# Folding x a second time, and the last transform product over the two halves of the array's rows

## The chip, the core and the metric

The kernel runs on one core of a Trainium2 chip. A core has a matrix engine (TensorE, "PE", with its weight loads shown apart as "PEld"), VectorE ("DVE"), ScalarE ("ACT"), GpSimd ("POOL") and SyncE ("SP"), which run side by side and wait for one another through semaphores. Data come from the chip's memory by DMA into SBUF; TensorE reads SBUF and writes PSUM[...]. The metric is the device time of one launch in microseconds, lower is better.

## What is computed

The reference is a Fourier mixing layer followed by a mixture-of-experts layer in which every token goes to one expert:

```python
def _attn_ref(x):                       # x: (8, 2496, 256), float32
    X = np.fft.fft(x, axis=1)
    X = np.fft.fft(X, axis=2)
    return X.real.astype(np.float32)

def _moe_ref(x, w_gate, w1, w2):        # x: (19968, 256), 8 experts, F = 1024
    logits = x @ w_gate
    expert_idx = np.argmax(logits, axis=1)
    ...
    gate_w = probs[np.arange(N), expert_idx]
    ...
    for e in range(E):
        lo, hi = (boundaries[e], boundaries[e + 1])
        h = np.maximum(x_sorted[lo:hi] @ w1[e], 0.0)
        y_sorted[lo:hi] = h @ w2[e]
    y = y_sorted[inv_perm]
    return (gate_w[:, None] * y).astype(np.float32)
```

`probs` is the softmax of the logits. The sequence length is 2496 = 104 x 24, so the transform along it is done in two steps, of 104 (`NA`) and of 24 (`NB`).

## The kernel before

The eight batches pass through a pipeline. While the experts work on the tokens of batch b - 1, the transform of batch b and the first stage of batch b + 1 are woven in between as side work.

**First stage** (`first`, `fold`, `fold_d`, `half1`). A batch's x comes in three thirds, each a tile `xq` of 104 partitions with eight rows of 256 numbers; three such tiles are in rotation (`xp`, tag `xq`). `fold` (L294) first adds the four mirrored rows of n2 to the other four (L301), then `fold_d` (L287) folds along d: positions 1 to 127 become the sum of d and 256 - d, positions 129 to 255 their difference, and 0 and 128 are copied (L290 to L292). These are VectorE operations. In the last third one row, `pm0`, is folded apart. `half1` (L306) multiplies the folded rows by the table `w1` over 104 partitions, ACT copies the product from PSUM (L316), and a DMA on SP or ACT writes it to `Td` in memory (L337), from where `regroup` (L346) reads it back with other rows on the partitions.

**Second stage** (`second`, L356). 53 positions of the sequence's spectrum (`NK`) are left after the fold, five to a group, so there are 11 groups (`NG`) in a batch. `turn_last(h)` (L360) turns one column of the regrouped tile `t4` by a small product with the table `rot` (tile `pr`) and copies the result back on ACT; there are two such tiles a batch. `group(g)` (L369) takes two products, over 120 partitions and with 120 columns, into a PSUM tile `p2`, and ACT copies it into `zz` (L374). In `zz` the partitions are the 128 folded positions of d, once for each of two parts c.

**Last stage**, the row product (loop at L391). Ten steps a batch (`NW`, 80 in the kernel) each take 128 columns of `zz` as weights and multiply them with the table `rd` into a PSUM tile `p3`: one product for each part c, over all 128 partitions and with 145 and 146 columns. The columns hold the half spectrum along d (129 values, `NY`), the gate's logits for two mirrored rows (2 x 8) and one column for the last position. ACT copies the second part to `zs` (L400). VectorE copies the logits out of `p3` (L403) and makes the two mirrored rows, as `p3 + last +/- zs` (L405). `mirror` (L378), on ACT, fills the other half of each row. After five steps `route` (L411) finds each row's expert and its place, and `send` (L457) lets POOL write each row to `Xs` by an indirect DMA (L230).

**Buffers.** `p2`, `p3`, the product of `half1`, `pr` and the small products of `route` share three PSUM buffers (`pm_`, tag `m`, `bufs=3`); the experts have the five others (`pse`).

**Experts** (`experts`, L627). Blocks of up to 512 rows are fetched from `Xs` with their expert's weights. Each is transposed (`pt`, L571) and multiplied with w1 (tiles a to e in blocks that use seven products in place of eight, `ph` in the others), then with w2 (`py`), scaled (L721) and scattered to the output (L230). At the end of the last round some blocks may be empty; `needed` (L635) then does a one-row product of ones in place of the block's work.

**The order** is written out by hand (`tc.manual_schedule()`). The loop at L824 draws from `experts` and, for the work that each step reports, lets so many ticks of the side work fall due:

```python
            if not full:
                due += TICKS * w / (SHARE * open_) if w else 1
            while due >= 1:
                next(side, None)
                due -= 1
                if b < LATE or not w:
                    send()
```

`TICKS` is 32 (L183) and `SHARE` 0.6. A tick is what lies between two `yield`s of `mixed` (L764), which advances `second(b)` by one step, and after every other step `first(b + 1)` as well. For batch 0 there is no expert work to weave with: its first stage, the first stage of batch 1 and its second stage run by themselves.

The tables are built on the host in `shape_consts` (L57): `rt`, `rd` and `alt` (a sign for each of 128 positions, by which the transposed rows are scaled at L572) depend on how d is folded.

Of the kernel before, what the change touches and what calls it, by code (L numbers as in the profile page):

```python
# [22 lines left out]
H = D // 2  # L23
# [16 lines left out]
ROWS = E * CAP + BLK  # L40
W = D + 2
NSL = 2 * HW
NY = H + 1
OUT = 1.0e6


def free(ap, offset, *dims):
    return bass.AP(ap.tensor, ap.offset + offset, [list(ap.ap[0])] + [list(d) for d in dims])
# [8 lines left out]
def shape_consts():  # L57

    c = {}
    n1 = np.arange(NA)[:, None]  # L60
    r = np.arange(NP)
    k1 = r // 2
    im = r % 2

    def wave(n2, f):
        return f(2 * np.pi / S * ((NB * n1 + n2) * k1 % S))

    w1 = [np.where(im, wave(n2, np.sin), wave(n2, np.cos)) for n2 in range(1, NS)]
    for f in (np.cos, np.sin):
        w1 += [np.where(im, 0.0, wave(0, f)), np.where(im, wave(NS, f), 0.0)]  # L70
    c["w1"] = np.stack(w1, 1) * (k1 < NK)

    u, cs, s = np.meshgrid(np.arange(NU), np.arange(2), np.arange(NS), indexing="ij")
    u, cs, s = (v.reshape(-1, 1) for v in (u, cs, s))
    k2 = np.arange(NB)
    t = 2 * np.pi / NB * ((s + 1) * k2 % NB)
    end = np.where(cs, 1.0 - 2.0 * (k2 % 2), 1.0)
    even = np.where(s == NS - 1, end, np.where(cs, -np.sin(t), np.cos(t)))
    odd = np.where(s == NS - 1, end, np.where(cs, np.cos(t), np.sin(t)))
    own = (u == np.arange(NU)).astype(float)  # L80
    c["m2"] = np.stack([(own[:, :, None] * m[:, None, :]).reshape(GP, GP) for m in (even, odd)], 1)

    rot = np.zeros((GP, GP))
    for p in range(GP):
        if p % NS == NS - 1:
            rot[p, p] = 1.0
        elif p // NS % 2:
            rot[p, p - NS] = -1.0
        else:
            rot[p, p + NS] = 1.0  # L90
    c["rot"] = rot

    d = np.arange(H)[:, None]
    m = np.arange(D + 1)
    t = 2 * np.pi / D * (d * m % D)
    rc, rs = np.cos(t), -np.sin(t)
    rs[0] = 1.0 - 2.0 * (m % 2)
    full = np.concatenate([rc[:, :D], rs[:, :D]], 0)


    rd = np.zeros((H, 2, 2 * E + NY + 1))
    sign = 1.0 - 2.0 * (m[:NY] % 2)
    rd[:, 0, 0:NY] = sign * rc[:, 0:NY]
    rs[0] = 0.0
    rd[0, 1, 2 * E] = 1.0
    rd[:, 1, 2 * E + 1:] = sign * rs[:, 0:NY]
    c["rd"] = rd
    c["alt"] = 1.0 - 2.0 * (np.arange(128) % 2)[:, None]
    c["rt"] = full.T.reshape(2, 128, D).transpose(1, 0, 2)

    p = np.arange(128)[:, None, None, None]
    h = np.arange(2)[None, :, None, None]
    g = np.arange(HW)[None, None, :, None]
    mir = np.arange(2)
    tau = 128 * (HW * h + g) + p
    k1 = tau // NB
    k = k1 + NA * (tau % NB)
    bad = (k1 >= NK) | ((mir == 1) & ((k1 == 0) | (k1 == NK - 1)))
    row = np.where(bad, 0, np.where(mir, S - k, k))
    c["row"] = row.reshape(128, 2, NSL)  # L120
    c["good"] = 1.0 - bad.reshape(128, 2, NSL)
    c["far"] = OUT * bad.reshape(128, 2, NSL)
    c["rev"] = np.broadcast_to(E - np.arange(E), (128, E))
    c["cap"] = np.broadcast_to(CAP * np.arange(E), (128, E))
    c["sgn"] = np.where(np.arange(128) == 0, 1.0, -1.0)[:, None]
    c["lane"] = np.arange(128)[:, None]
    c["tri"] = np.triu(np.ones((128, 128)), 1)
    c["ident"] = np.eye(128)
    return {n: np.ascontiguousarray(v, dtype=np.float32) for n, v in c.items()}
# [50 lines left out]
    return todo  # L180


TICKS = 32  # L183
LATE = 4
SHARE, ROOM = 0.6, 1.2
WARM = 16
# [23 lines left out]
def kernel(ctx: ExitStack, tc, x, w_gate, w1, w2, out):  # L210
# [3 lines left out]
    def mm(o, lhsT, rhs, start=True, stop=True, **kw):  # L214
        nc.tensor.matmul(o, lhsT=lhsT, rhs=rhs, start=start, stop=stop, **kw)  # L215
# [71 lines left out]
    def fold_d(o, a, n):  # L287

        lo, hi = free(a, 1, [D, n], [1, H - 1]), free(a, D - 1, [D, n], [-1, H - 1])
        vec.tensor_tensor(free(o, 1, [D, n], [1, H - 1]), lo, hi, op=ALU.add)  # L290
        vec.tensor_tensor(free(o, H + 1, [D, n], [1, H - 1]), lo, hi, op=ALU.subtract)
        vec.tensor_copy(free(o, 0, [D, n], [H, 2]), free(a, 0, [D, n], [H, 2]))  # L292

    def fold(xq, q, pm0):  # L294

        a, m = xq[:, 0:4], xq[:, 4:8]
        n = 4
        if q == NQ - 1:
            n = 3
            fold_d(pm0, m[:, 3], 1)  # L300
        vec.tensor_tensor(a[:, 0:n], a[:, 0:n], m[:, 0:n], op=ALU.add)  # L301
        yield
        fold_d(m, a, 4)
        yield

    def half1(b, q, half, pm, pm0, t1):  # L306
# [13 lines left out]
    def first(b):  # L320

        pm0 = xp.tile([NA, D], F32, tag="pm0", name="pm0")
        for q in range(NQ + 1):
            f = iter(())
            if q < NQ:
                xq = ahead.pop((b, q))
                f = fold(xq, q, pm0[:])
            next(f, None)
            yield
            if q:  # L330
                t1 = xp.tile([NP, 4, D], F32, tag="t1", name="t1")
                half1(b, q - 1, 0, pm, pm0, t1)
            next(f, None)
            yield
            if q:
                half1(b, q - 1, 1, pm, pm0, t1)
                (nc.sync if b > 1 else act).dma_start(out=Td[b][:, 4 * (q - 1) * D:4 * q * D], in_=t1[:].rearrange("p j d -> p (j d)"))  # L337
                if b:
                    load(b + 1, q - 1)
            next(f, None)  # L340
            pm = xq[:, 4:8]
            yield

    base = con["cap"]
# [11 lines left out]
    def second(b):  # L356

        t4 = None

        def turn_last(h):  # L360

            nonlocal t4
            t4 = ahead.pop((b, "t4", h))
            n = min(HALF, NG - h * HALF)
            pr = pm_.tile([GP, HALF], F32, tag="m", name="pr")
            mm(pr[:, 0:n], con["rot"][:], t4[0:GP, 0:n, H])
            act.copy(t4[0:GP, 0:n, H], pr[:, 0:n])  # L367

        def group(g):  # L369
            i, n = g % HALF, LAST if g == NG - 1 else GP  # L370
            p2 = pm_.tile([128, 2, n], F32, tag="m", name="p2")
            for c in range(2):
                mm(p2[:, c], t4[0:GP, i, c * H:(c + 1) * H], con["m2"][:, c, 0:n])
            act.copy(zz[:, :, g * GP:g * GP + n], p2[:])  # L374
            if g == HALF - 1:
                turn_last(1)

        def mirror(rows, k):  # L378
            act.copy(free(rows[:], (k + 1) * W + D - 1, [-W, 2], [-1, H - 1]),
                     free(rows[:], k * W + 1, [W, 2], [1, H - 1]))  # L380

        turn_last(0)
        yield
        group(0)
        yield
        group(1)
        yield
        for h in range(2):
            rows = sp.tile([128, NSL, W], F32, tag="rows", name="rows")
            lg = sp.tile([128, NSL, E], F32, tag="lg", name="lg")  # L390
            for i in range(HW):  # L391
                w, k = HW * h + i, 2 * i
                if w + 2 < NG:
                    group(w + 2)
                p3 = pm_.tile([128, 2 * NY + 2 * E + 1], F32, tag="m", name="p3")
                z = zz[:, :, 128 * w:128 * (w + 1)]
                mm(p3[:, 0:NY + 2 * E], z[:, 0], con["rd"][:, 0, 0:NY + 2 * E], True, False, skip_group_check=True)
                mm(p3[:, NY:], z[:, 1], con["rd"][:, 1], False, True, skip_group_check=True)
                zs = sp.tile([128, NY + 1], F32, tag="zs", name="zs")
                act.copy(zs[:], p3[:, NY + 2 * E:])  # L400
                if i:
                    mirror(rows, k - 2)
                vec.tensor_copy(lg[:, k:k + 2], p3[:, NY:NY + 2 * E].rearrange("p (m e) -> p m e", m=2))  # L403
                for m, op in enumerate((ALU.add, ALU.subtract)):
                    vec.scalar_tensor_tensor(rows[:, k + m, 0:NY], p3[:, 0:NY], zs[:, 0:1], zs[:, 1:],  # L405
                                             op0=ALU.add, op1=op)
                yield
            mirror(rows, k)
            yield from route(b, h, rows, lg)
# [354 lines left out]
    def mixed(b):  # L764

        one, two = (ahead_of(b + 1) if b + 1 < B else iter(())), second(b)
        for _ in range(3):
            next(one, None)
            yield
        for k, _ in enumerate(two):  # L770
            if k % 2:
                next(one, None)
            yield
        yield from woven(close(b), one)
        yield from through(b)
# [129 lines left out]
```

## Time and profile before

| | us |
|---|---|
| median of three runs | 1346.6 |
| lowest, highest | 1344.01, 1350.37 |
| the profiled execution | 1317.19 |
| its span, first to last instruction | 1314.9 |

The profiled execution is a single one and lies under the timed runs; what is counted up from its trace is compared with its own time. Its mean granted TensorE clock was 0.978 of full speed. A line of the trace gives the start and the duration in microseconds, the engine, the line of the kernel, the operation, the tile written and the tiles read, their shape, and a count if several of the kind follow one another. In the chain of waits, each line is a piece of the chain of work that ended last. All matrix work is recorded at L215, the helper `mm`, so its lines are told apart by the tiles. Each float32 product appears as two matmul instructions with two weight loads. Durations of matmuls overlap, since they are pipelined; what one costs is seen from start to start.

The work of the parts that the change touches, by the groups of the trace:

| what | count | mean, ns |
|---|---|---|
| row product, 145 and 146 columns (`p<-table,zz`) | 160 and 160 | 310 and 294 |
| group product, 120 columns (`p<-table,t`) | 320 | 291 |
| ACT copy to `zs` (L400), 128x130 | 80 | 268 |
| DVE logits (L403), 128x16 | 80 | 173 |
| DVE rows (L405), 128x129 | 160 | 343 |
| DVE fold along d (L290, L291), 104x508 | 24 and 24 | 683 and 679 |

### The profile page before, as it was taken

To read this page: it belongs to the slowest core of one execution; us is meant where nothing else is said; L and a number is where in the kernel's file an instruction comes from. 1 tells how busy PE (TensorE), PEld (TensorE's weight loads), DVE (VectorE), ACT (ScalarE), POOL (GpSimd) and SP (SyncE) were. 2 spreads that over 40 slices of the span, in tenths; PEclk is the share of its full clock that TensorE was granted. 3 is DMA by queue.
4 is the path that set the end of the run, shared out by engine and by line. 5 is a ranking of instruction groups with operands and counts; after the bars stand their busy time and mean duration, and the time that the engine had idled before them with its cause. 6 is when DMAs were issued, how large, how long until landed. Compare 5 with 4: busy or idle time off the path is not lost.

```text
span 1314.9 us, 19479 instructions
## 1 busy us (share of the span) xinstructions
PE 1270.8 (97%) x6823; PEld 1105.0 (84%) x6823; DVE 620.8 (47%) x1610; ACT 386.4 (29%) x907; POOL 330.6 (25%) x335
## 2 busy tenths in 40 slices
PE   5769999999999999999999999999999999999998
PEld 4659988776888888888888888888888889999887
DVE  4654253352656535664556644575544342222442
ACT  1422141231244223433334322432332231212221
POOL 0336125043114411153112511144211111111111
PEclk6869999999999999999999999999999999999999
DMA  8878967455436522574332633243432237777785
GB/s 245 268 240 302 389 213 247 160 171 188 182 134 205 199 104 97 176 267 131 145 111 81 244 115 105 97 159 133 155 138 101 97 133 262 277 270 260 274 324 196
DMA packets 63101, 249.65 MB, mean 190 GB/s; under 512 B 10057, under 2 KB 24883, under 8 KB 43420
## 3 DMA queue, kind: packets, MB, share of 16 engines
q1 hardware_dynamic: 46231, 203.33, 44.5%
q0 software_dynamic: 15888, 42.14, 8.8%
q10 hardware_dynamic: 885, 2.94, 0.7%
q8 instruction: 55, 0.90, 0.3%
q14 instruction: 42, 0.34, 0.1%
HBM read 194.97 MB, written 54.83 MB: 190 GB/s over the span
## 4 chain that ended last, share of the span: by engine, by line
PE 91%; issue 1%; DMA 1%; DVE 1%; ACT 0%; POOL 0%; POOLq 0%; SPq 0%; ACTq 0%
PE py L215 42%; PE ph L215 12%; PE c L215 8%; PE a L215 8%; PE p L215 5%; PE b L215 4%; PE e L215 4%; PE d L215 4%; PE pt L571 3%; PE s L215 2%; DMA xb<-Xs 0%; PE rk L215 0%; DMA Xs<-rows,pi 0%; DVE xq L301 0%; ACT y L721 0%
## 5 line engine op out<-in xcount | busy, mean ns | idle before, releaser
L215 PE MATMUL py<-w_sb,hT 128*128 128x256 f32 x2560 | 578.0, 380 | 0.0
L215 PEld LDWEIGHTS py<-w_sb,hT 128*128 128x128 f32 x2560 | 477.8, 190 | 60.5
L230 POOL DMA_INDIRECT out_dram<-y,ro x163 | 160.5, 985 | 806.4 <-ACT y L721 699.3
L721 ACT ACTIVATE y<-py,xb 128x256 f32<-128x256 f32 x163 | 77.2, 474 | 494.7 <-PE py L215 494.3
L230 POOL DMA_INDIRECT Xs<-rows,pi x160 | 162.1, 1013 | 172.4 <-DVE rows L405 52.7
L215 PE MATMUL ph<-xT,w_sb 128*128 128x128 f32 (+2 forms) x992 | 170.8, 328 | 2.9 <-ACT y L721 2.1
L215 PEld LDWEIGHTS ph<-xT,w_sb 128*128 128x128 f32 x992 | 136.6, 192 | 27.9 <-issue 17.2
L698 DVE TENSOR_SCALAR hT<-ph 128x512 f32<-128x512 f32 x49 | 33.9, 691 | 226.9 <-PE ph L215 109.9
L604 DVE TENSOR_TENSOR u<-p,b 128x512 f32<-128x512 f32 x57 | 39.2, 688 | 188.7 <-PE b L215 173.7
L215 PE MATMUL a<-xT,w_sb 128*128 128x256 f32 (+1 forms) x512 | 117.4, 356 | 0.0
L215 PEld LDWEIGHTS a<-xT,w_sb 128*128 128x128 f32 x512 | 89.7, 190 | 10.3
L572 DVE TENSOR_SCALAR xT<-pt,table 128x512 f32<-128x512 f32 (+1 forms) x94 | 63.3, 674 | 49.4 <-PE pt L571 49.2
L614 ACT ACTIVATE hT<-a 128x512 f32<-128x512 f32 x57 | 34.0, 597 | 152.1 <-PE a L215 152.1
L215 PE MATMUL s<-xq,w 104*112 104x256 f32 (+2 forms) x208 | 61.9, 421 | 11.8 <-DVE xq L292 11.3
L403 DVE COPY lg<-p 128x16 f32<-128x16 f32 x80 | 13.8, 173 | 120.2 <-ACT zs L400 120.1
L571 PE MATMUL pt<-table,xb 128*128 128x128 f32 x326 | 53.6, 280 | 9.4 <-DMA xb<-Xs 9.4
L215 PEld LDWEIGHTS p<-table,t 120*128 120x128 f32 x352 | 54.1, 203 | 9.1 <-issue 2.4
L215 PE MATMUL p<-table,zz 128*128 128x145 f32 (+1 forms) x320 | 57.0, 302 | 3.7 <-DVE rows L405 2.8
L215 PE MATMUL p<-table,t 120*128 120x120 f32 (+1 forms) x352 | 57.9, 289 | 1.7 <-ACT t L367 1.1
L215 PE MATMUL b<-xs,ws 128*128 128x256 f32 (+1 forms) x256 | 58.7, 356 | 0.0
L215 PE MATMUL d<-xT,w_sb 128*128 128x256 f32 (+1 forms) x256 | 58.7, 356 | 0.0
L215 PE MATMUL e<-xs,w_sb 128*128 128x256 f32 (+1 forms) x256 | 58.7, 356 | 0.0
(115 smaller groups left out, 1356.4 us busy)
## 6 DMA issues: line engine op xcount, KB each, us to landing
w_sb<-in_moe_w_dram SPq DMA_DIRECT2D x132, 1024.0 KB, 8.0
xq<-in_x_dram SPq DMA_DIRECT2D x24, 896.0 KB, 9.2
xb<-Xs SPq DMA_DIRECT2D x28, 516.0 KB, 3.8
Td<-t SPq DMA_DIRECT2D x18, 448.0 KB, 3.3
t<-Td SPq DMA_DIRECT2D x8, 768.0 KB, 12.0
t<-Td SPq DMA_DIRECT2D x8, 640.0 KB, 14.2
xb<-Xs SPq DMA_DIRECT2D x13, 258.0 KB, 3.1
xb<-Xs SPq DMA_DIRECT2D x25, 129.0 KB, 3.0
```

The costliest lines, as they stand in the source:

```text
L215: nc.tensor.matmul(o, lhsT=lhsT, rhs=rhs, start=start, stop=stop, **kw)
L230: return unordered(pool.indirect_dma_start(out=dst, out_offset=bass.IndirectOffsetOnAxis(ap=idx, axis=0), in_=rows, in_offset=None, bounds ...
L403: vec.tensor_copy(lg[:, k:k + 2], p3[:, NY:NY + 2 * E].rearrange("p (m e) -> p m e", m=2))
L571: nc.tensor.transpose(pt[:, c, t], xb[:, 2 * h + t, c * 128:(c + 1) * 128], ident[:])
L572: vec.tensor_scalar(xT[:, :, 256 * h:256 * h + 128 * n], pt[:].rearrange("p c t k -> p c (t k)"), con["alt"][:], None, op0=ALU.mult)
L604: vec.tensor_tensor(u2[:], p1[:], b[:], op=add)
L614: act.activation(h11, a[:], ACTF.Relu)
L698: vec.tensor_scalar(o, ph[:], 0.0, None, op0=ALU.max)
L721: act.activation(y[:], py[:], ACTF.Copy, scale=xb[:, i, D + 1:D + 2])
```

## The change

x is folded a second time along d, d with 128 - d (`fold_q`), so that the rows of `zz` hold in partitions 0 to 63 what the even positions of the spectrum need and in 64 to 127 what the odd ones need. The folded rows go back into the first four rows of `xq`; in the last third of a batch `pm0` is folded twice as well, by way of a second tile with its tag.

The row product of a step becomes four products over 64 partitions each: for each part c one over partitions 0 to 63 into a PSUM tile `even` and one over 64 to 127 into a tile `odd`, with 81 columns in the first part and 82 in the second (`NY` is now 65). ACT copies both tiles, 147 columns each, to `zs`; VectorE then reads SBUF only. The logits are the sum of the two tiles' parts; the even positions of the two rows are made by two fused operations over 65 columns, the odd ones by two plain ones over 64, each written with a stride of two.

The second rotation, `turn_last(1)`, moves out of `group` to a tick of its own, a tick before the group that needs it. In `mixed` a step of `first` gets its own tick, and `TICKS` goes from 32 to 45. The tables `rd`, `rt` and `alt` follow the new order of d.

```diff
+Q = H // 2
+NY = Q + 1
...
-TICKS = 32
+TICKS = 45
...
+    def fold_q(o, a, n):
+        for k, first, at, (one, other) in ((Q, 0, 0, (ALU.add, ALU.subtract)),
+                                           (Q - 1, H + 1, H + 1, (ALU.subtract, ALU.add))):
+            lo, hi = free(a, first, [D, n], [1, k]), free(a, H if first == 0 else D - 1, [D, n], [-1, k])
+            vec.tensor_tensor(free(o, at, [D, n], [1, k]), lo, hi, op=one)
+            vec.tensor_tensor(free(o, at + k, [D, n], [1, k]), lo, hi, op=other)
+        vec.tensor_copy(free(o, H, [D, n], [H - 1, 2]), free(a, Q, [D, n], [H, 2]))
...
         if q == NQ - 1:
             n = 3
-            fold_d(pm0, m[:, 3], 1)
+            t = xp.tile([NA, D], F32, tag="pm0", name="pm0")
+            fold_d(t[:], m[:, 3], 1)
+            fold_q(pm0, t[:], 1)
         vec.tensor_tensor(a[:, 0:n], a[:, 0:n], m[:, 0:n], op=ALU.add)
         yield
         fold_d(m, a, 4)
+        fold_q(a, m, 4)
         yield
...
             act.copy(zz[:, :, g * GP:g * GP + n], p2[:])
-            if g == HALF - 1:
-                turn_last(1)
...
+                if w + 2 == HALF:
+                    turn_last(1)
+                    yield
                 if w + 2 < NG:
                     group(w + 2)
-                p3 = pm_.tile([128, 2 * NY + 2 * E + 1], F32, tag="m", name="p3")
                 z = zz[:, :, 128 * w:128 * (w + 1)]
-                mm(p3[:, 0:NY + 2 * E], z[:, 0], con["rd"][:, 0, 0:NY + 2 * E], True, False, skip_group_check=True)
-                mm(p3[:, NY:], z[:, 1], con["rd"][:, 1], False, True, skip_group_check=True)
-                zs = sp.tile([128, NY + 1], F32, tag="zs", name="zs")
-                act.copy(zs[:], p3[:, NY + 2 * E:])
+                even, odd = (pm_.tile([128, 2 * NY + 2 * E + 1], F32, tag="m", name="p3") for _ in range(2))
+                for c in range(2):
+                    for o, at in ((even, 0), (odd, Q)):
+                        to = slice(0, NY + 2 * E) if c == 0 else slice(NY, None)
+                        rd = con["rd"][at:at + Q, c, 0:to.stop]
+                        mm(o[:, to], z[at:at + Q, c], rd, c == 0, c == 1, skip_group_check=True)
+                zs = sp.tile([128, 2, 2 * NY + 2 * E + 1], F32, tag="zs", name="zs")
+                act.copy(zs[:, 0], even[:])
+                act.copy(zs[:, 1], odd[:])
                 if i:
                     mirror(rows, k - 2)
-                vec.tensor_copy(lg[:, k:k + 2], p3[:, NY:NY + 2 * E].rearrange("p (m e) -> p m e", m=2))
+                gate = zs[:, :, NY:NY + 2 * E].rearrange("p o (m e) -> p o m e", m=2)
+                vec.tensor_tensor(lg[:, k:k + 2], gate[:, 0], gate[:, 1], op=ALU.add)
+                last = zs[:, 0, NY + 2 * E:NY + 2 * E + 1]
                 for m, op in enumerate((ALU.add, ALU.subtract)):
-                    vec.scalar_tensor_tensor(rows[:, k + m, 0:NY], p3[:, 0:NY], zs[:, 0:1], zs[:, 1:],
-                                             op0=ALU.add, op1=op)
+                    vec.scalar_tensor_tensor(free(rows[:, k + m], 0, [2, NY]), zs[:, 0, 0:NY], last,
+                                             zs[:, 0, NY + 2 * E + 1:], op0=ALU.add, op1=op)
+                for m, op in enumerate((ALU.add, ALU.subtract)):
+                    vec.tensor_tensor(free(rows[:, k + m], 1, [2, Q]), zs[:, 1, 0:Q],
+                                      zs[:, 1, NY + 2 * E + 1:2 * NY + 2 * E], op=op)
                 yield
...
         for k, _ in enumerate(two):
             if k % 2:
+                yield
                 next(one, None)
             yield
```

## The prediction

> **What bounds the kernel now.** First the page's busy shares and the busy time of the engines by stretches of the span.
>
> ```profile
> PE 1270.8 (97%) x6823; PEld 1105.0 (84%) x6823; DVE 620.8 (47%) x1610; ACT 386.4 (29%) x907; POOL 330.6 (25%) x335
> ...
> 61.00:114.00 53.00, 41.63 (x213) 35.25 (x213) 29.71 (x120) 15.22 (x45) 23.32 (x22) 0.76 0.77 253
> ...
> 429.50:581.60 152.10, 151.91 (x782) 133.41 (x781) 85.41 (x205) 53.43 (x133) 40.09 (x40) 1.00 0.45 158
> ```
>
> A row of the second part gives a stretch, its length, then PE, PEld, DVE, ACT, POOL busy, granted clock, DMA share and GB/s. Up to 114 us PE has holes; from there it is full (151.91 of 152.10 us in one batch's period). So there are two regimes: in the start a chain through DVE and DMA sets the time, later every PE nanosecond of a batch's side work is a nanosecond of the kernel. The chain of waits shows the second regime.
>
> ```profile
> 429.52 10.36 PE py L215 x48
> ...
> 456.44 10.36 PE py L215 x48
> ...
> 550.38 0.95 PE p L215 x8
> ...
> 581.60 10.36 PE py L215 x48
> ```
>
> A batch takes 581.60 - 429.52 = 152.08 us. A block without side work takes 456.44 - 429.52 = 26.92 us. One 128-row step of the transform's last stages (eight instructions, group product and row product) takes 0.95 us. The timeline splits it:
>
> ```profile
> 542.38 0.60 PE L215 MATMUL p<-table,t 120*128 120x120 f32 x4
> 542.82 0.67 PE L215 MATMUL p<-table,zz 128*128 128x145 f32 x4
> 543.33 1.89 PE L215 MATMUL py<-w_sb,hT 128*128 128x256 f32 x8
> ...
> 527.27 0.28 PE L215 MATMUL pr<-t,table 120*120 120x5 f32 x2
> 527.41 0.74 PE L215 MATMUL p<-table,zz 128*128 128x145 f32 x4
> 527.99 1.03 PE L215 MATMUL a<-xT,w_sb 128*128 128x256 f32 x4
> ```
>
> Start to start, since durations overlap: each f32 product is two instructions here. The row product (zz) holds PE 543.33 - 542.82 = 0.51 us for four, 128 ns each; the group product (t) 0.44, 109 each. The rotation pr has only 5 columns, yet it and the following zz take 527.99 - 527.27 = 0.72, so pr costs 0.21, 105 ns each: below some 120 columns the column count stops mattering and the weight load sets the price.
>
> **What the Trainium skill says.** "TensorE: Matmul & The Clock Gate", section "LDWEIGHTS (loading the stationary operand)": the load takes P/1.2 ns with P the columns, whatever the rows. For 128 that is an estimate of 107 ns; the trace's 109 (group) and 105 (rotation) agree. The same page, "Part 3: Packing small matmuls — row/col tiling", "The mechanism": matmuls on different row groups run side by side, a load overlaps a running matmul only where the row group differs, and matmuls start in order. "TensorEngine Tiling (Array Packing)", "Key Properties": tiles load and multiply independently, but a change of tiling mode drains TensorE. No run here shows two row tiles yet. Of a change of height the trace has one example, blocks at the end whose work is skipped and replaced by one-row products:
>
> ```profile
> 1240.34 0.38 PE L215 MATMUL py<-w_sb,hT 128*128 128x256 f32 x1
> ...
> 1240.65 0.60 PE L215 MATMUL ph<-ones 1*128 1x512 bf16 x2
> ...
> 1241.18 0.44 PE L571 MATMUL pt<-table,xb 128*128 128x128 f32 x2
> ...
> 1241.55 0.28 PE L215 MATMUL py<-ones 1*128 1x256 bf16 x1
> ```
>
> A py instruction streams 0.216 us (the chain's 10.36/48), so it is through at 1240.56, and the one-row product starts 0.09 later. The two of that take 0.60 - 0.38 = 0.22 apart, so are through at 1241.09; the next starts 0.09 later. The two pt stream 0.11 each (0.44/4 of the group product), until 1241.40; the next starts 0.15 later. So a change of height costs 0.1 us or somewhat more, where 128-row products of different kinds follow without a gap. A branch lies at these places too, so part may be the branch.
>
> **The change part by part.** *Row product, per step.* Removed: 4 instructions, 0.51 us. Added: four products, 8 instructions of 64 rows and 81 or 82 columns. By columns (0.51/4 for 145.5, thus 0.88 ns a column) one streams 0.07 us, under the load's 0.109. If the halves ran fully side by side, four slots of 0.109 make 0.44; one after the other, eight make 0.87. The order is even, odd, even, odd, with the two instructions of a product adjacent and on the same rows. Only the second of one product can pair with the first of the next: slots e1, e2+o1, o2+e3, e4+o3, o4, five of 0.109 = 0.55. I take that. The steps lie between 128-row group products, so two changes of height per step: none at best, 0.2 each at worst (0.1 of gap, and 0.1 of uncovered weight load: zz after a wait shows 0.77 instead of 0.67 for four). I take 0.1 each, as measured. Sum 0.55 + 0.20 - 0.51 = +0.24 per step. Of the 80 steps 66 lie after 85 us (264 of 320 zz instructions), where PE is the bound: 66 x 0.24 = +15.8 us. The 14 earlier ones lie in PE's holes: 0.
>
> *Second fold.* DVE streams f32 from SBUF start to start, not by its durations:
>
> ```profile
> 512.57 0.42 DVE L557 TENSOR_TENSOR xs<-xT,xs 128x256 f32<-128x256 f32 x1
> 512.91 0.42 DVE L558 TENSOR_TENSOR xT<-xT 128x256 f32<-128x256 f32 x1
> ...
> 42.32 0.17 DVE L403 COPY lg<-p 128x16 f32<-128x16 f32 x1
> 42.40 0.60 DVE L405 SCALAR_TENSOR_TENSOR rows<-p,zs 128x129 f32<-128x129 f32 x2
> 42.92 0.16 DVE L403 COPY lg<-p 128x16 f32<-128x16 f32 x1
> ```
>
> 256 elements take 512.91 - 512.57 = 0.34; the first fold's 508 take 0.60 (9.11 to about 9.72). Four operations of 256 and a small copy: 4 x 0.34 + 0.1 = 1.45 per third of a batch; the last third has four more of 64 elements, 0.14 each by the same line, so 0.65. In all 24 x 1.45 + 8 x 0.65 = 40 us of DVE. Rows: 42.32 to 42.92, 0.60 per step, become an addition (0.09), two fused ones of 65 (0.17 each) and two plain ones of 64 (0.14 each), 0.71, so +9 us in all. DVE goes from 621 to about 670 us, hidden in the full stretch behind PE; if a fold burst (2.7 us, now 4.1) stands before the rows that a mirror copy on ACT waits for, evictions behind it are late: 0 to +8 us, I take +1.
>
> *The start.* There the same work is exposed. The first products wait for the folds, the rows for batch 1's last fold, and the first block for its rows:
>
> ```profile
> PE s L215 <- DVE xq L292: 11.3, 4, 5.6
> PE pt L571 <- DMA xb<-Xs: 9.4, 2, 7.1
> ...
> PE p L215 <- DVE rows L405: 3.4, 3, 2.0
> ```
>
> Batch 0's last third starts on its DMA (18.0 us), so only its own 1.45 + 0.65 = 2.1 is late. Batch 1's last third does its fold at 39.58 to 42.32, right ahead of the first rows, and adds another 2.1, with 0.5 for five steps of 0.11: some +4.5 us on the route, then on POOL's row sends, which run back to back from 53.1, then on the first block's load. Bounds +2 (the row buffers now come free after ACT alone, so the 3.4 us waits go) and +7 (all of batch 1's folds).
>
> *The rest.* ACT copies two tiles of 147 instead of one of 130: 0.27 becomes 2 x 0.28, +23 us over the kernel, on an engine that is 29% busy; it also frees the PSUM buffers one step later in line, three per step from a pool of three, but two full steps back to back still find the first copy done. The second rotation has a tick of its own: between 114 and 1041 us PE waited 1.1 us in all for the copy after such a rotation (ACT t L367), so -1. The ticks: 19 + 3 + about 4 of side work over 32, and about 37 over 45, end at the same 0.82; 0. No DMA is added or moved on SP's or POOL's queue.
>
> Sum: 15.8 + 4.5 + 1 - 1 = +20.3 us on the profiled 1317.2 (span 1314.9 and 2.3 around it), 1337.5. The median of the runs stands 29.4 above that execution; I add the same difference to it: 1346.6 + 20.3 = 1367.
>
> **The rivals.** *No overlap:* both halves share one weight path. 0.87 + 0.2 - 0.51 = 0.56 x 66 = 37, with the start 41: 1388 (1401 at 0.2 per change of height). For it: nothing measured shows two loads at once. Against: the skill's independent tiles. *No difference:* full overlap and free changes: (0.44 - 0.51) x 66 = -4.6, against +4.5 of the start: 1346. *Faster:* the place is the row product of the full stretch, the mechanism that each half's load is hidden beside the other half's streams too, so the load is no floor: four slots of 0.07 make 0.28, -0.23 x 66 = -15, with +4.5 of the start -10.7: 1336. It decides from a cost below 0.51 - (6.7 + 4.5)/66 = 0.34 us per step. Against it: pr's 105 ns and the one-row gaps. For it: half of the multiplications are gone, and PE is the bound. That the change doesn't do what it says, 64-row products kept in full-height mode, is the no-overlap case without the gaps: 1375.
>
> **How the numbers follow.** Forecast 0.41, no overlap 0.22, no difference 0.15, faster 0.22. This measurement tells about 0.5%, 6.7 us. So slower 0.63, within 0.15, faster 0.22; the likeliest case's own range is 1356 to 1380, and the whole one 1335 to 1392, which leaves out the far ends.
>
> **What would show it.** The timeline from a group product to what follows the row product: 0.75 us for the eight instructions (0.87 or more: no overlap; 0.34 or less: faster); a gap of 0.1 us at either end of it; a batch's period 152.1 + 10 x 0.24 = 154.5 us; the first block's pt near 90 instead of 85.3 us. I am wrong if the period shrinks, or if the holes come from ACT or DVE instead.

## The result, and the profile after

The changed kernel takes 1391.78 us (median of four runs, 1388.89 to 1400.59) beside 1345.3 for the kernel before (four runs, 1343.67 to 1350.37): ratio 1.035, interval 1.0295 to 1.0405, so slower by 46 us. The profiled execution is one of these runs, 1392.66 us with a span of 1390.9. Unlike the profile of the kernel before, which lies 29 us under its timed runs, it stands next to its median. That turns out to matter.

The busy times of the whole span, first part of the page of after:

```profile
PE 1315.6 (95%) x7143; PEld 1128.5 (81%) x7143; DVE 675.9 (49%) x1930; ACT 405.4 (29%) x987; POOL 332.9 (24%) x335
```

DVE is 55 us busier than before (forecast about 50) and ACT 19 (forecast 23), both still under half of the span. PE has 320 instructions more and 45 us more of recorded time.

Stretches of after (columns as in the prediction: stretch, length, PE, PEld, DVE, ACT, POOL, granted clock, DMA share, GB/s):

```profile
61.00:114.00 53.00, 31.30 (x167) 26.08 (x167) 29.48 (x132) 13.55 (x45) 21.33 (x20) 0.58 0.68 241
114.00:200.00 86.00, 80.27 (x480) 70.37 (x479) 34.39 (x131) 19.40 (x50) 27.35 (x28) 0.94 0.76 259
200.00:290.00 90.00, 78.01 (x402) 63.52 (x401) 34.59 (x141) 20.98 (x59) 27.44 (x28) 0.89 0.59 198
429.50:581.60 152.10, 151.93 (x802) 131.98 (x800) 89.88 (x231) 54.00 (x134) 40.18 (x40) 1.00 0.45 157
```

The second and third stretch in the kernel before:

```profile
114.00:200.00 86.00, 84.18 (x509) 75.97 (x506) 34.33 (x120) 22.45 (x58) 27.49 (x29) 1.00 0.81 297
200.00:290.00 90.00, 87.73 (x428) 69.19 (x427) 34.84 (x117) 24.42 (x63) 31.23 (x33) 0.98 0.58 195
```

In the last row of after PE is as full as before (151.93 of 152.10 us), so the second regime still holds. New are the second and third rows: between 114 and 290 us, where the forecast took PE to be full, it lacks 5.7 and 12.0 us, where the kernel before lacked 1.8 and 2.3. In the first row the clock is 0.58, where it was 0.76 in the profile before, and PE does 167 instructions where it did 213.

The chain of waits of after (start, duration, piece) shows both:

```profile
150.54 11.32 another core or an unknown queue
...
246.68 11.89 another core or an unknown queue
...
489.73 10.36 PE py L222 x48
...
516.64 10.36 PE py L222 x48
...
644.84 10.36 PE py L222 x48
```

A block without side work still takes 516.64 - 489.73 = 26.91 us. A batch takes 644.84 - 489.73 = 155.11 in place of 152.08: +3.03 us for ten steps of the last stages. And there are two pieces of 11 us which the chain puts down to no engine of this core; what the second is, is told below. In the first PE is busy for 10.17 of the 12 us from 150 to 162.

The timeline of PE in after, two steps one behind the other (start, duration, instruction):

```profile
580.63 0.60 PE L222 MATMUL p<-table,t 120*128 120x120 f32 x4
581.16 0.68 PE L222 MATMUL p<-table,zz 64*128 64x81 f32 x8
581.77 0.70 PE L222 MATMUL p<-table,t 120*128 120x120 f32 x4
582.40 0.68 PE L222 MATMUL p<-table,zz 64*128 64x81 f32 x8
583.01 1.99 PE L222 MATMUL py<-w_sb,hT 128*128 128x256 f32 x8
584.84 1.03 PE L222 MATMUL s<-xq,w 104*112 104x256 f32 x4
```

Start to start, the group product takes 581.16 - 580.63 = 0.53 (0.44 before): 0.09 of it is a gap on the way into the 64-row products. The eight instructions take 581.77 - 581.16 = 0.61, with the gap on the way out in it. The second group product, which follows such a row product, takes 582.40 - 581.77 = 0.63, another 0.1 more; so do the eight of py, 584.84 - 583.01 = 1.83 where 8 x 0.216 are 1.73. Whatever comes first after the switch back pays it. Inside the eight, the distance from one start to the next alternates between 6 or 7 ns and 105 or 106 ns, with 167 ns once at the beginning: four slots of about 0.112 us from pair to pair, longer in the first, with two instructions in each. A step of both products costs 0.30 more than before (3.03 / 10).

The trace doesn't name the half of an instruction, but semaphores and column counts show that a pair has one of each, and that they don't start in program order. The program gives even, odd, even, odd, two instructions each; the last of either half in the second part raises a semaphore, so those two stand sixth and eighth. In 70 of the 80 steps they start seventh and eighth. In the other ten an instruction of 82 columns, thus of the second part, starts ahead of the last one of 81. So each half seems to go through its own work without waiting for the other's turn.

One of those ten comes in each of the three full batches. It is longer, as in the changed kernel on another chip (`a_same` of the experiments):

```profile
539.69 0.59 ACT L336 COPY t<-s 112x512 f32<-112x512 f32 x1 [1.97 <-PE s L222]
540.03 0.98 PE L222 MATMUL p<-table,zz 64*128 64x81 f32 x8
540.93 0.48 PE L222 MATMUL py<-w_sb,hT 128*128 128x256 f32 x1
```

This step takes 540.93 - 540.03 = 0.90 in place of 0.61. The first stage's product `s`, `p2`, `even` and `odd` are four tiles for three PSUM buffers. ACT's copy of `s` ends at 540.28, and the first load of the odd half starts at 540.33. So 0.3 us a batch are a wait for ACT.

PE's waits in after (what waits, for what: total us, times, longest):

```profile
PE pt L601 <- DMA xb<-Xs: 11.9, 1, 11.9
PE s L222 <- DVE xq L309: 11.5, 3, 6.7
```

The waits for `rows` (3.4 us before) are gone, as forecast; PE waits for the first block's rows 11.9 us in place of 9.4, until 99.26 us instead of 85.32.

### The profile page after: what moved, and what is told of

Same layout as the page of the kernel before. It is cut to its first block, busy times and chain, and to the rows that moved or that the text cites. A ratio compares the mean times of both kernels' runs of the same rounds, so it can differ in the third digit from the quotient of the medians.

```text
span 1390.9 us, 20507 instructions
## 1 busy us (share of the span) xinstructions
PE 1315.6 (95%) x7143; PEld 1128.5 (81%) x7143; DVE 675.9 (49%) x1930; ACT 405.4 (29%) x987; POOL 332.9 (24%) x335
## 4 chain that ended last, share of the span: by engine, by line
PE 86%; DVE 6%; issue 2%; DMA 2%; another core or an unknown queue 2%; ACT 1%; POOL 0%; POOLq 0%; SPq 0%; DVEq 0%; ACTq 0%
PE py L222 37%; PE ph L222 11%; PE p L222 7%; PE a L222 7%; PE c L222 7%; PE e L222 4%; PE d L222 3%; PE b L222 3%; PE pt L601 3%; PE s L222 3%; DMA xq<-in_x_dram 1%; DVE xq L307 0%; DVE xq L308 0%; DMA Xs<-rows,pi 0%
## 5 line engine op out<-in xcount | busy, mean ns | idle before, releaser
L222 PE MATMUL ph<-xT,w_sb 128*128 128x128 f32 (+2 forms) x992 | 182.6, 341 | 13.6 <-DVE hT L728 4.7
L222 PEld LDWEIGHTS ph<-xT,w_sb 128*128 128x128 f32 x992 | 141.9, 199 | 43.4 <-issue 21.7
L222 PE MATMUL s<-xq,w 104*112 104x256 f32 (+2 forms) x208 | 65.5, 440 | 22.4 <-DVE xq L309 11.5
L429 DVE TENSOR_TENSOR lg<-zs 128x16 f32<-128x16 f32 x80 | 14.1, 176 | 130.6 <-ACT zs L425 106.9
L222 PEld LDWEIGHTS s<-xq,w 104*112 104x112 f32 x208 | 40.4, 211 | 34.4 <-issue 13.2
L222 PE MATMUL p<-table,zz 64*128 64x81 f32 (+1 forms) x640 | 63.7, 309 | 4.4 <-issue 2.9
L601 PE MATMUL pt<-table,xb 128*128 128x128 f32 x326 | 54.5, 284 | 12.2 <-DMA xb<-Xs 11.9
L222 PE MATMUL p<-table,t 120*128 120x120 f32 (+1 forms) x352 | 62.2, 304 | 3.0 <-ACT zz L394 2.5
L222 PEld LDWEIGHTS p<-table,zz 64*128 64x128 f32 x640 | 50.4, 204 | 16.8 <-issue 6.4
L222 PE MATMUL c<-xT,ws 128*128 128x256 f32 (+1 forms) x256 | 58.9, 357 | 4.3 <-DVE hT L640 2.6
```

The costliest lines, as they stand in the source:

```text
L429: vec.tensor_tensor(lg[:, k:k + 2], gate[:, 0], gate[:, 1], op=ALU.add)
L601: nc.tensor.transpose(pt[:, c, t], xb[:, 2 * h + t, c * 128:(c + 1) * 128], ident[:])
```

## The experiments

*The theories.* T1, tiling: the 64-row products cost the time, through the change of tiling mode (from 128 rows of the array to halves of 64 and back) and the slots between. T2, the second fold and the rows: VectorE's extra work delays the start and the evictions. T3, the schedule: new ticks put side work in worse places. T4 came up on the way: part of the difference goes with the chip and not with the change alone.

**The same two kernels on other chips.** No edit. The kernel before ran four times with a profile, the changed one twice.

> The kernel before, unchanged, profiled beside the others. Its first profile (1317 us) lies 28 us under its timed runs, the changed kernel's does not. Theory A (the chip's DMA state stalls the first rounds in any kernel): this profile is near 1345 and shows waits of several us between 114 and 300 us, where the first one was full. Theory B (the change alone makes the early holes): near 1317 and PE full from 114 us on.

> The kernel before, unchanged, profiled on the same chip as the three that follow (so far two chips were used: one on which it takes 1317 us, one on which it takes 1345). Theory A, that the slower chip stalls all kernels alike in the early rounds: on that chip its trace shows the 28 us as holes in PE before 360 us. On the faster chip: 1317 again, PE full from 114 us.

> The kernel before, unchanged, for a profile on the chip of this call. On the slower chip (1345 us): 27 us of holes before 390 us, which answer to those of the changed kernel there. On a faster one: 1317 again.

> The kernel before, unchanged. On the slower chip: holes of 27 us before 390 us. On another: 1317 again.

> The changed kernel, unchanged. In the last runs the kernel before took 1317 us, not the 1345 beside which the change was first timed. By the parts measured so far (full height product +9.9 us over before, of which the fold 7.4, the ticks -1.6, the wider product 66 x 0.06 = 4), and 66 x (0.70 - 0.57) = 8.6 us for the tiling: 1336 us, ratio 1.014. If the early holes of its first profile (some 25 to 30 us between 114 and 360 us) belong to the change: 1360 or more, ratio 1.03.

> The changed kernel on this chip. Theory A (the chip's stalls come on top, the change's own cost is the product, the fold and the start): on the faster chip 1336 us; on the slower one 1395 again, of which the kernel before on that chip shows 28 us too. Theory B (the change makes the early holes on any chip): 1360 or more on the faster chip too.

Where two numbers stand for a kernel, the first is the median of its timed runs and the second its profiled run.

| chip | the kernel before, us | the changed kernel, us | ratio (interval) |
|---|---|---|---|
| of the result | 1345.3 | 1391.78 | 1.035 (1.0295 to 1.0405) |
| 2 | 1344.81 | 1395.09 (`a_again`) | 1.0376 (1.0332 to 1.042) |
| 13 | 1344.06; 1346.89 (`b_fourth`) | | |
| 6 | 1318.14; 1318.68 (`b_same`) | 1342.7 (`a_same`) | 1.0192 (1.0145 to 1.0239) |
| 3 | 1317.36; 1322.42 (`b_again`) | | |
| 14 | 1319.24; 1317.13 (`b_third`) | | |

The chips fall into two kinds. On chips 3, 6 and 14 the kernel before takes 1317 to 1319 us; on 2, on 13 and on that of the result, which has no number on record and may be one of these two, 1344 to 1345. The changed kernel loses 24.5 us on the one kind (chip 6 alone, three runs) and 46 to 50 on the other; the intervals of the ratios don't touch. Each chip was used at one time only, so what is called a kind here may be a property of the chip or a state of that hour.

The traces tell the kinds apart as well. Those of the first hold 13,257 to 13,511 records of a semaphore being raised, those of the second 10,649 to 11,094, although no instruction is missing. By this mark the profile that the prediction was built on (1317.19 us, 13,263 records) is of the first kind, and the profile of the result (11,006) of the second.

In the full stretch the kinds don't differ. The chain of the changed kernel on chip 6 (`a_same`):

```profile
443.52 10.36 PE py L222 x48
...
598.63 10.36 PE py L222 x48
```

598.63 - 443.52 = 155.11, the same as on the chip of the result; the kernel before has 152.07 on chip 6. What differs lies nearly all before 390 us. The kernel before, on chip 6 (`b_same`) and then on chip 13 (`b_fourth`), by stretches:

```profile
213.00:226.00 13.00, 13.00 (x64) 11.45 (x63) 2.12 (x4) 1.88 (x4) 9.95 (x11) 1.00 1.03 390
200.00:290.00 90.00, 87.96 (x437) 69.78 (x436) 37.59 (x130) 24.55 (x65) 30.18 (x31) 1.00 0.57 195
```

```profile
219.00:232.00 13.00, 4.30 (x12) 2.90 (x10) 0.00 (x0) 0.60 (x1) 9.16 (x10) 0.74 1.04 389
200.00:290.00 90.00, 79.31 (x371) 63.29 (x370) 30.32 (x97) 19.68 (x51) 24.76 (x26) 0.92 0.53 184
```

The upper rows are the same piece of work, a burst in which weights, x and the rows sent by POOL move at once. The DMA engines are full in both and move the same 390 GB/s, and POOL sends ten or eleven times. On chip 6 PE works through it without a hole; on chip 13 it is busy 4.30 of 13 us and DVE not at all. In after, the second of the two pieces of its chain is such a hole, at a DMA share of 0.72 (start, duration, instruction; in brackets the idle time before it and its releaser, `remote` where no instruction of this core ended close to the release):

```profile
246.47 0.21 DVE L711 CAST ro<-xb 128x2 int32<-128x2 f32 x1
...
250.17 0.60 ACT L730 ACTIVATE hT<-ph 128x512 f32<-128x512 f32 x1 [6.52 <-remote]
...
250.82 3.78 PE L222 MATMUL ph<-xT,w_sb 128*128 128x256 f32 x8 [4.23 <-issue]
...
258.59 0.69 DVE L728 TENSOR_SCALAR hT<-ph 128x512 f32<-128x512 f32 x1 [11.91 <-remote]
```

DVE reads what PE wrote until 250.82 + 3.78 = 254.60, yet starts 4 us later, at 258.59; ACT starts 3.6 us after the end of the matmul that it reads (246.59). The semaphores name the engine that they waited for. Both waits are for the semaphore that PE raises, and the trace has it raised at 250.15 and 258.56, just ahead of the two starts; PE then waits for ACT in turn. So it is PE that reports late, and the others stand still behind it. In the thirteen traces of the first kind PE raises it within 0.2 us of the recorded end of a matmul, up to the last one of the span. In the six of the second kind it comes more than 1 us late 16 to 27 times, by up to 7.9 us, all but at most two of them before 400 us. In after, ACT and DVE raise theirs within 0.03 us. The ends of matmuls in a trace are modelled, so whether PE worked late or only reported late isn't shown.

For the kernel before, these holes make 28 us (`b_fourth` against `b_same`, by the span): its first tile of py is no later (104.87 us beside 105.56), and 26 us have gathered when the first full batch begins. The changed kernel has more of them: against the kernel before on the second kind (`a_again` against `b_fourth`) it is 11.8 us late at the first tile of py, 36 when the first full batch begins, and then falls behind by 3.03 us a batch, as on the first kind, until 48. On chip 6 the same three readings are 3.0, 12.3 and 24. So of the 24 us that the second kind adds, 9 arise before the first tile of py and 15 from there to the first full batch.

**The second fold alone.** The kernel before with the second fold added on VectorE; its results aren't read by anything. `fold_q` is that of the change.

```diff
             fold_d(pm0, m[:, 3], 1)
+            t = xp.tile([NA, D], F32, tag="pm0", name="pm0")
+            fold_q(t[:], pm0, 1)
...
         fold_d(m, a, 4)
+        fold_q(a, m, 4)
```

> The kernel before with the second fold's VectorE operations done as well, into rows that nothing reads; row product and ticks as before. If the fold on VectorE is what makes the start and the first rounds late: +15 to +30 us. If, as the prediction had it, it is hidden but for the start: +2 to +6 us.

> The kernel before with the second fold unread, on this chip. On the faster chip: +7 us again. If the slower chip makes the same work dearer, since its early rounds wait on DMA with DVE in the chain: +15 us or more there.

`b_fold` takes 1325.8 us on chip 3 (ratio 1.0056, 1.0041 to 1.007) and `b_fold_same` 1325.66 on chip 6 (1.0045, 1.0029 to 1.0061): 6 to 8 us. In `b_fold01` the fold is added in batches 0 and 1 alone, those that are folded with little or no expert work to weave with (chip 13).

> The kernel before with the second fold on VectorE, unread, in batches 0 and 1 only. If the fold costs in the start alone, as the prediction had it: the same 7 us as with all batches. If it costs in all rounds by standing before other VectorE work: 2 us.

It takes 1349.34 us (1.0043, 1.0024 to 1.0063), 5.3 us more than the kernel before. The two chips are of different kinds, so the two sums are only roughly comparable, but they agree with a price that is mostly paid in the start. Later the fold is nearly hidden: a batch of `b_fold_same` takes 152.28 us beside 152.07. So T2 holds for the start, and hardly beyond it.

**The schedule alone.** The kernel before with the change's ticks (`b_sched`, repeated on another chip as `b_sched_more`), and the changed kernel with the old ones (`a_sched`).

```diff
-TICKS = 32
+TICKS = 45
...
-            if g == HALF - 1:
-                turn_last(1)
...
+                if w + 2 == HALF:
+                    turn_last(1)
+                    yield
...
+                yield
```

> The kernel before with the ticks of the change (45, the extra yields, the second rotation on a tick of its own) and nothing else. If the spreading of the side work is what costs in the early rounds: +8 us or more. If not: within 3 us of before.

> The kernel before with the change's ticks. A gain of 1.6 us was measured; its batch period is 0.55 us shorter, four batches of it 2.2 us. If it is real: 1 to 3 us under before again.

> The changed kernel with the ticks of before (32, no extra yields, the second rotation inside the group). If three PSUM buffers a step in ticks that follow each other cost waits on ACT's copies: 5 us or more over the changed kernel. If the ticks don't matter, as in the kernel before: within 3 us of it.

`b_sched` takes 1315.7 us (0.9982, 0.9974 to 0.9991) and `b_sched_more` 1341.5 (0.998, 0.9962 to 0.9999): 1.7 and 2.6 us faster than the kernel before, with a batch of 151.52 us. It is the one version that beats both kernels; the interval of the second only just leaves out no change. `a_sched` takes 1392.79 us on chip 2, 2.3 under `a_again`, too little to tell from it (its ratio to the kernel before is 1.0362, 1.0315 to 1.041). T3 falls: the ticks cost nothing in either kernel.

**The change without the tiling.** All of the change but for the row product: this has 128 rows again, with a table that holds zeros where the other half's rows are, and two products of 162 and 164 columns into one PSUM tile. The lines that build the table and copy the tile are left out here.

```diff
-                    for o, at in ((even, 0), (odd, Q)):
-                        to = slice(0, NY + 2 * E) if c == 0 else slice(NY, None)
-                        rd = con["rd"][at:at + Q, c, 0:to.stop]
-                        mm(o[:, to], z[at:at + Q, c], rd, c == 0, c == 1, skip_group_check=True)
+                    to = slice(0, NY + 2 * E) if c == 0 else slice(NY, None)
+                    rd = con["rd"][:, c].rearrange("p (o m) -> p o m", o=2)[:, :, 0:to.stop]
+                    mm(p3[:, :, to], z[:, c], rd, c == 0, c == 1, skip_group_check=True)
```

> The changed kernel with the row product over all 128 partitions again: the same two folds, the same 162 and 164 columns, zeros in the table where the other half's rows are, two products in place of four and no change of tiling. The trace of the changed kernel gives 0.70 us for a step's row product with the gap ahead of it, this one should take 4 x 0.143 = 0.57. If the tiling's drains are the main cost: 9 to 14 us under the changed kernel (about 1380). If they are nearly all of it: 1355 or less. If they aren't: no less than 1388.

> The full height product with the rest of the change, on this chip. On the faster chip it took 1327 us. If the row tiling has 46 us of its own, it stays within 12 us of the kernel before on either chip; if it is only 9 us, it lies 9 us under the changed kernel on the same chip.

`a_full` takes 1327.22 us (1.0069, 1.0043 to 1.0095) on chip 3 and `a_full_same` 1325.55 (1.0055, 1.0039 to 1.0071) on chip 6. The timeline of `a_full_same`:

```profile
524.63 0.60 PE L222 MATMUL p<-table,t 120*128 120x120 f32 x4
525.07 0.72 PE L222 MATMUL p<-table,zz 128*128 128x162 f32 x4
525.63 0.60 PE L222 MATMUL p<-table,t 120*128 120x120 f32 x4
526.07 0.73 PE L222 MATMUL p<-table,zz 128*128 128x162 f32 x4
```

The group product takes 0.44 again and the row product 525.63 - 525.07 = 0.56, against 0.51 for the narrower one. A batch takes 152.65 us, 0.58 more than before, and ten times 0.05 to 0.06 for the wider products is about that. The ticks take some 0.55 off a batch (`b_sched`), so fold, rows and copies together cost about as much, 0.06 a step, and no more: T1 holds in the full stretch. The tiling is 1342.7 - 1325.55 = 17.2 us on chip 6 (three runs of the changed kernel, up to 1348.57, so this is good to a few us), and by the wider products' 66 x 0.06 = 4 more against the row product of before: 21 of the 24.5.

**The change of tiling mode, alone.** Both kernels add to each step of the changed kernel one small product over 128 rows with 8 columns, which nothing reads. In `a_ahead` it stands ahead of the four, beside the group product; in `a_mid` between the products of the two parts, so that a step has one more pair of changes and is else the same. Both widen the two PSUM tiles by 8 columns, which isn't shown here.

```diff
# a_ahead
+                mm(odd[:, WP:], con["ident"], z[:, 0, 0:8], True, False, skip_group_check=True)
                 for c in range(2):
# a_mid
                 for c in range(2):
+                    if c:
+                        mm(odd[:, WP:], con["ident"], z[:, 0, 0:8], False, False, skip_group_check=True)
```

> The same small product ahead of the four, beside the group product, where it adds no change of tiling: 66 x 0.21 = 14 us over the changed kernel. The difference of a_mid to this is the price of a pair of changes: 23 us if it is 0.35 us, under 5 if they are cheap.

> The changed kernel with one small 128-row product of 8 columns, which nothing reads, between the first and the second part's products of every step: two more changes of tiling a step. If a pair of changes costs the 0.35 us that the trace gives (0.51 + 0.29 of growth - 0.45 of four slots): 66 x (0.35 + 0.21 of the product itself) = 37 us over the changed kernel. If the changes are cheap and the halves' products are what costs: 14 us (the product alone) to 18.

On chip 14 `a_ahead` takes 1358.79 us (1.0308, 1.0264 to 1.0352) and `a_mid` 1390.32 (1.0542, 1.0497 to 1.0586). A step of `a_ahead` and then one of `a_mid`, from a group product to the next:

```profile
547.63 0.60 PE L223 MATMUL p<-table,t 120*128 120x120 f32 x4
548.07 0.29 PE L223 MATMUL p<-zz,table 128*128 128x8 f32 x2
548.30 0.68 PE L223 MATMUL p<-table,zz 64*128 64x81 f32 x8
548.90 0.70 PE L223 MATMUL p<-table,t 120*128 120x120 f32 x4
```

```profile
569.39 0.60 PE L223 MATMUL p<-table,t 120*128 120x120 f32 x4
569.92 0.45 PE L223 MATMUL p<-table,zz 64*128 64x81 f32 x4
570.30 0.39 PE L223 MATMUL p<-zz,table 128*128 128x8 f32 x2
570.62 0.45 PE L223 MATMUL p<-table,zz 64*128 64x82 f32 x4
571.00 0.70 PE L223 MATMUL p<-table,t 120*128 120x120 f32 x4
```

548.90 - 547.63 = 1.27 and 571.00 - 569.39 = 1.61. The period of a batch says the same; the chain of `a_ahead` and then that of `a_mid`:

```profile
456.60 10.36 PE py L223 x48
...
612.99 10.36 PE py L223 x48
```

```profile
478.00 10.36 PE py L223 x48
...
637.89 10.36 PE py L223 x48
```

With 156.39 and 159.89 us the extra pair costs 3.50 / 10 = 0.350 us. That agrees with the changed kernel's own row: 0.51 of the old product + 0.30 lost - 0.45 of the four slots = 0.36. The whole kernels lie 31.5 us apart, where 23 was expected: 66 x 0.35 = 23 from the steps, and 7.6 because the first tile of py comes at 122.72 us in place of 115.13. In `a_ahead` the gap of 0.09 has moved from the group product (0.44 again) to behind the small one, so it belongs to the change of mode and not to what stands there.

**Sends that keep pace.** The holes lie where POOL sends rows back to back. With `LATE = 1` the rows of the later rounds are sent as the side work falls due.

```diff
-LATE = 4
+LATE = 1
```

> The changed kernel with the row sends of rounds 1 to 3 paced as those of the later rounds. If bursts of sends hold the engines up on the slower chip: 10 to 25 us under the changed kernel there (1392). On a faster chip, where no holes are: within 3 us of 1343.

It takes 1394.36 us (1.0582, 1.0536 to 1.0627) on chip 14, a chip of the first kind, which has no holes to take away: some 52 us more than the changed kernel on chip 6, where no difference was expected. PE's waits in `a_late1` from 110 to 430 us:

```profile
PE pt L601 <- DMA xb<-Xs: 41.1, 3, 16.5
```

Now the expert blocks wait 41.1 us for their rows. That costs more than the holes do, and on the holes of the second kind the run says nothing, for it wasn't made there.

## Why the prediction went as it did

The direction and, for the full stretch, the mechanism were right: PE's side work there is the kernel's time, and a step of it got longer. The size was 46 us instead of 20. The step that failed is the last of the sum, where the distance between one profile and the timed runs was carried over to the changed kernel as a constant. The result lies nearest to the rival without overlap (1388), but by luck: its mechanism is refuted, for it had the eight instructions at 0.87 us, and they take 0.61. Point by point:

- *Overlap of the halves* ("slots e1, e2+o1, o2+e3, e4+o3, o4, five of 0.109 = 0.55"): four slots, 0.45, as in the prediction's own case of halves fully side by side. The five came from starts in program order, which "TensorE: Matmul & The Clock Gate", Part 3, "The mechanism", states as well. The trace agrees with that page in that matmuls on different row groups run side by side, 6 or 7 ns apart, but not in the order: in 70 of 80 steps the sixth instruction of the program starts seventh, and here the measurement decides. The rival that lets the load vanish (four slots of 0.07) is refuted by the same number.
- *Change of tiling* ("I take 0.1 each, as measured"): mis-sized. Measured 0.350 us a pair, so 0.175 each, near the upper end of 0.2 that the prediction kept. "TensorEngine Tiling (Array Packing)", "Key Properties", says that a change of mode drains TensorE; the runs put the price to it. The blocks of ones showed only the gap before the start, not the slower first instructions behind it. That the two errors partly cancel is luck: 0.45 + 0.35 - 0.51 = 0.29, measured 0.30, forecast 0.24.
- *66 steps x 0.24 = 15.8 us*: with 0.30 it is 20 us. The experiment has 21.
- *The start, +4.5*: fits on the first kind of chip, as far as it can be read. The first tile of py comes 3.0 us later on chip 6, the first pt at 91.64 us in place of 87.74 there (forecast near 90 from 85.3), and the fold alone delays the first tile of py by 2.2 to 3.3 (the three kernels with the fold, each against the kernel before on its chip). But the kernel before itself has that tile anywhere from 101.94 to 105.56 us in its four profiles of the first kind. On the second kind of chip it is 11.8 us.
- *VectorE's bursts +1, the rotation's tick -1*: no run takes them apart; all the ticks together give -1.7 and -2.6. That three PSUM buffers a step from a pool of three cost nothing was not quite so: 0.3 us a batch.
- *"The median of the runs stands 29.4 above that execution; I add the same difference to it"*: this is the step that failed. The 29.4 us were taken as a constant. They are the distance between the two kinds of chip, 28 us of idle stretches in the first rounds, and the changed kernel loses some 24 us more to them there: 48 us (`a_again` against `b_fourth`) where chip 6 has 24. On chip 6 the change measures +24.5 (by the interval of its ratio, 1.0145 to 1.0239, 19 to 32) against the +20.3 of the sum, which that interval holds. So the sum was right or a little short, and the constant was wrong by the rest.

What sets the holes stays open. Shown is where they are (in the first rounds, on one kind of chip; the one of `b_fourth` in a burst that fills the DMA engines, the one of after at a share of 0.72), that they begin with PE's semaphore being raised late, and that more is lost to them with the change. The traces with holes are also those in which records of semaphores are missing; whether the recording has a part in the holes no run tells. In the start of after the clock granted was also lower (a mean of 0.58 between 61 and 114 us, on chip 6 0.66 with the change and 0.71 without); whether that is a cause or a consequence of PE's idle time isn't shown. Nor is it whether the change loses more because its start is later, or because its side work falls elsewhere among the bursts; the ticks (`a_sched`, 2.3 us) don't account for it.

## What to carry to other kernels

Splitting a product into row halves gains little here: the four slots shrink only from 0.128 to 0.112 us each, though the columns go from 145 to 81, and every passage from full-height products to half-height ones and back costs 0.35 us. By these numbers a step saves 0.51 - 0.45 = 0.06 us, so some six steps would have to share one passage to make it up; that is an estimate, and no run tried it. And where a single profile stands away from the median of the runs, what makes the difference is to be found before a change is priced in it: the gap need not be the same for the changed kernel.

## What was not expected of the hardware

- A pair of changes between 128-row and 64-row products costs 0.350 us, of which 0.09 is an empty gap ahead of the first 64-row product.
- Row halves overlap: in most steps instructions of the two halves start 6 or 7 ns apart, a pair every 0.112 us. Matmuls of different row halves don't keep program order (70 of 80 steps).
- The same kernel takes 2% longer on some chips (1344 to 1345 us) than on others (1317 to 1319). The same burst at 390 GB/s leaves PE busy 13.00 of 13 us on one and 4.30 on another. PE's semaphore is then raised up to 7.9 us after the recorded end of its matmul; on the faster chips it never is more than 0.2 us late before the end of the span.
